# Softcap attention and a two-layer network on one core: P kept in f32 for two more pairs, exponentials turned unscaled, split scores on row halves, the cap in registers

## The chip, the cores and the metric

One Trainium2 chip, one of its cores. The time is the device time of one execution in microseconds (us). The kernel before takes 695.26 us (median of 3 runs, 694.31 to 695.97). Engines in the text: PE is TensorE, DVE VectorE, ACT ScalarE, POOL GpSimd, SP the engine that issues the DMAs.

## The reference, cut to what matters

```
q, k, v: (4, 12, 448, 64) f32            # batch, heads, tokens, head width
s = q @ k.T / 8;  s = cap * tanh(s / cap)
p = exp(s - max(s));  p = p / (sum(p) + 1e-9)
x = p @ v, heads side by side            # (4*448, 768)
h = x @ w_in                             # 768 -> 2048
g = where(h > 0, h, alpha * h)           # alpha per column of h
out = g @ w_out                          # 2048 -> 768
```

## The kernel before, in words

Every product has to come out with the accuracy of f32. The kernel has two ways to get it. Either the operands stay f32 and PE takes several passes over each product (a product is then two matmul records in the trace), or each operand is split into an f16 high part and an f16 low part (`hi`, `lo`) and PE forms three f16 products (high by high, high by low, low by high).

The work is 12 units in batch 0 (6 pairs of heads by two parts of the tokens, 384 and 64 of them: `PART`) and 18 units in batches 1 to 3 (one pair of heads with all 448 tokens each). `steps` (L532) goes through a unit in steps of two blocks of 128 rows of scores (one head each); the last step of a 448-token unit has one block that holds 64 rows of each head. A step is: scores on PE, tanh on ACT (L553), row maxima on DVE (L558), the bias of the exponential (L560), exponential with its row sums on ACT (L565), then 1/sum on POOL and DVE (L570, L573), and then P is turned, since P @ V needs P with the keys on the partitions.

- Scores of batches 0 and 1 are f32 (`scores_32`, L520): a head's 64 columns of q and k stand on one half of PE's rows, and the two heads' products are meant to run side by side. In batches 2 and 3 q and k are split, and `nat` holds (q high, q low), (k high, k high), (k low, k low); one DMA transpose makes `qkTs` of it, and `split_scores` (L780) makes two matmuls of all 128 rows per block (L785).
- P of batch 0 is turned on PE by `turn_32` (L602): four f32 matmuls of P by a diagonal matrix of 1/sum, `diags` (made at L607), so that the turn also divides. The turned P is copied from PSUM (L621), and `PV_32` (L657) multiplies it by V in f32.
- P of batches 1 to 3 is scaled, split into f16 high and low (`turn_split`, L582) and turned by DMA (L598); V is split (`split_v`), and `PV_split` (L642) makes 24 f16 matmuls per unit.

Each unit's output is scaled and split by `xout` into `xring`, and the network goes on from there: `mm1` (L806) is x @ w_in, `mm2` (L847) is g @ w_out, both in three f16 products. The weights are loaded, put together as f32 (L902 to L912), bounded by their column norms (`norms`, L919: products on PE, L926, and a maximum on DVE, L931), scaled and split.

The order on each engine is written out ahead of time: every operation is recorded with a priority, a dependency list and an assumed duration, and `Plan.order` (L133) runs through them and gives each free engine the ready operation of lowest priority. The constants at the top of the file (`PEN`, `B0_P`, ...) and the table `OFF` shift the priorities. Where the plan sees PE without work ahead of `FILL_END`, it puts in a filler, a matmul of the identity by itself (`fill`, L1063) that nobody reads.

Of the kernel before, what the change touches and what calls it, by code (L numbers as in the profile page):

```python
# [24 lines left out]
GUARD = 1e-9 * math.exp(EXP_BIAS)  # L25
PD_A = 6
PD_B = 6
MQ = 3
AQ = 3
PEN = 4509.92  # L30
PEN2 = -1345.18
PENP = 6482.25
B0_P = -50.35
LD_P = -35.85
LO_P = 301.38
MM_P = 3324.02
X_P = 53.71
ST_P = 19.81
ST1_P = 13.45
PV_P = 374.14  # L40
QK_P = -32.7
V_P = -1.09
WI_P = 40.03
WI_S = -0.97
A_S = 13.05
MM1_P = 198.89
WO_P = 329.05
WO_S = -16.5
WT_P = -1461.61
WT_S = -141.91  # L50
B1_P = 277.05
B_S = 241.79
EVAC_P = -145.66
# [14 lines left out]
QA = 0.5  # L68
VA = 1.0
FS = [0, 6]  # L70
TURN = 95.0
TURN_P = 905.0
SCORE = 1040.0
# [5 lines left out]
OFF = [34.6, 0.4, 29.9, -6.1, 0.0, 1.5, -90.6, 40.5, 0.0, 0.0, -257.7, 0.0, 2.6, -1.0, 26.8, -8.5, -42.6, 107.4, 10.3, 125.2, 8.6, -267.5, -58.1, 2.0, -9.3, 235.7, 4.8, -32.5, 207.0, 194.2, 463.8, 229.6, 0.0, -31.2, -255.6, -6.9, -24.3, 57.8, -178.1, 70.7, 0.0, 225.2, -115.2, -52.7, 0.0, -130.7, 63.2, 240.7, 63.4, -111.4, 0.0, 0.0, 9.4, 97.8, -60.1, -181.2, -100.1, -35.7, 137.8, 0.0, -6.1, -78.0, -257.2, 31.2, -2.2, -147.9, 21.3, -0.4, 0.0, 21.9, 119.4, -148.7, 89.0, -63.5, 14.5, 76.1, -40.7, -49.1, 31.5, -2.8, 125.9, -8.9, 99.3, -23.6, -83.9, 175.4, 11.7, 163.5, -170.9, 0.0, 13.5, 0.2, -5.3, 0.2, -132.0, -577.9, -1.6, 9.7, -185.1, -10.0, 15.0, -245.3, 0.0, -22.7, 32.7, 149.3, -1091.5, -40.3, 0.0, -672.3, 15.6, -127.9, -897.3, 55.4, -59.5, 0.0, 167.9, 2.2, 12.5, -39.1, 123.8, -60.7, -437.0, -54.8, -543.8, -541.5, 4.4, 0.0, -1.4, -92.4, -0.7, -60.4, 150.0, 75.5, -504.3, 26.7, 69.5, 182.6, -11.4, -57.0, 55.8, 95.6, -4.2, 2.6, 230.8, 0.0, -572.4, 62.6, 1.6, -54.4, 0.0, -3.0, 20.2, 99.9, 396.1, 2.6]  # L79
# [9 lines left out]
class Plan:  # L89
# [43 lines left out]
    def order(self):  # L133
# [8 lines left out]
        port = {"dve": 0.0, "pool": 0.0}  # L142
# [46 lines left out]
        while todo:  # L189
# [10 lines left out]
            for e in free:  # L200
# [3 lines left out]
                while ready[e]:  # L204
# [20 lines left out]
                    elif e == "pe":  # L225
                        free[e] = run_pe(t, o.rows)
# [36 lines left out]
def kernel(  # L263
# [72 lines left out]
    nat = ct([P, 6 * NCH, P], F16, "nat")  # L336
    qkTs = ct([P, 2, 6 * NCH, CP], F16, "qkTs")
    aux = qkTs[:, 1].rearrange("p g t -> p (g t)").bitcast(F32)
    qzs = [aux[:, :512], aux[:, 512:1024]]
    qzr = [(("qkT", 1), 0, 512), (("qkT", 1), 512, 1024)]  # L340
# [3 lines left out]
    diags = ct([P, 4, P], F32, "diags")  # L344
# [4 lines left out]
    ams = ct([P, 3, 8], F32, "ams")  # L349
    vam = ct([P, 2, 2 * NPAIR], F32, "vam")  # L350
# [111 lines left out]
    def vbatch(b):  # L462
# [18 lines left out]
        first, *rest = pow2(u.inv, u.s, None)  # L481
        allmax(prio, u.vmx, P, [(u.tok, 6, 7)], first, [(u.tok, 7, 9)])
# [49 lines left out]
    def steps(u, prio, n, S_, s_ns, sr_, scale, dma):  # L532
# [4 lines left out]
        for i0 in range(0, nb, 2):  # L537
# [15 lines left out]
            op(pr, {"act": 245 + 377 * m}, lambda e, s=s, t=t, m=m: nc.scalar.activation(  # L553
                out=t, in_=s[:, :m, :S].rearrange("p c (j k) -> p c j k", j=NCH), func=AF.Tanh, scale=scale[0]),
# [47 lines left out]
    def turn_32(u, pr, n, c, t, tr, f, fr):  # L602

        i = dg_no[0] % 4
        dg_no[0] += 1
        d, dr = diags[:, i], ("dg", i, i + 1)
        op(pr, either(P, f=True, pool=True), lambda e: scaled(e, d, ident, f), r=[identr, fr], w=[dr])  # L607
        h = plan.handle("a")

        def turn_P(e):  # L610
# [24 lines left out]
    def split_v(u, prio, rv, rvt):  # L635
        vs = vs16[:CP, u.idx % 2]
        vt = [(("vs", u.idx % 2), z, z + 1) for z in range(2)]
# [4 lines left out]
    def PV_split(u, prio, n, vs, vt):  # L642
# [11 lines left out]
        op(prio, {"pe": TURN + 12 * (n / 2.4 + 12)}, PV, r=vt + [("pt", u.po[x], u.po[x] + 4 * n) for x in range(2)], w=[h])  # L654
        return h

    def PV_32(u, prio, n, vt, vr):  # L657
        h = plan.handle("a")

        def PV(e):  # L660
            pv = ps_p[h.slot]
# [6 lines left out]
        op(prio, {"pe": 4 * (n / 0.6 + 30) + 50}, PV, r=[("pt", u.po[0], u.po[0] + 8 * n), vr, (vb[u.b].tok, 7, 9)], w=[h], rows=0.875)  # L668
        return h
# [15 lines left out]
    def attention32(part, pair):  # L685
# [18 lines left out]
        op(prio, {"pe": TURN + 205 * nch}, lambda e, h=h: turn(h, rq, c0, nch), r=[rqr, identr], w=[h, qr], rows=0.7)  # L704
        op(prio, either(n, True), lambda e, h=h: copy(e, qz, ps_p[h.slot][:, o - c0 * CP:o - c0 * CP + n]), r=[h], w=[qr], port=False)
        dma = pair >= (PD_A, PD_B)[part]
# [4 lines left out]
        else:  # L711
            u.po = [po, po + n]
            u.pt = pt32[:CP, po:po + 8 * n].rearrange("p (j t) -> p j t", j=NCH)
            u.pv = [u.pt[:, :, y * n:(y + 1) * n] for y in range(2)]
        steps(u, prio, n, scores_32(qz, kt[:, pair], n), lambda blocks: SCORE, [qr, ktr], [icap], dma)
# [8 lines left out]
        else:  # L724
            xout(u, prio + X_P, h, n, o, vb[0].s, [(vb[0].tok, 7, 9)])


    def attention(b, pair):
# [11 lines left out]
        qkT = qkTs[:, u.idx % 2]  # L740
        qt = (("qkT", u.idx % 2), 0, 1344)
        if scores32:
            both = qkT.rearrange("p g t -> p (g t)").bitcast(F32)
            qz, kz = both[:, :S], both[:, S:2 * S]
            for i, raw, rr_, dst in ((14, rk, rkr, kz), (13, rq, rqr, qz)):
                h = plan.handle("a")
                w = (qt[0], (i - 13) * S, (i - 12) * S)
                op(prio - i, {"pe": TURN + 205 * NCH}, lambda e, h=h, raw=raw: turn(h, raw, 0, NCH), r=[rr_, identr], w=[h, w], rows=0.7)
                op(prio - i, either(S, True), lambda e, h=h, dst=dst: copy(e, dst, ps_p[h.slot][:, :S]), r=[h], w=[w], port=False)
        else:  # L750
# [10 lines left out]
            nq, nk, nl = (nat[:CP, 2 * NCH * i:2 * NCH * (i + 1)] for i in range(3))  # L761
            q4, k4 = (t.rearrange("p (c d) -> p c d", d=D) for t in (rq, rk))
            nt = [("nat", i * 512, i * 512 + 512) for i in range(3)]
            pr = prio - 13
            split(pr, q4, rqr, s[:CP, 0:1], amt, nq[:, :, 0:D], nt[0], nq[:, :, D:], nt[0], share(2 * u.idx, QA))
# [342 lines left out]
```

## Time and profile before

| | |
|---|---|
| median of 3 runs | 695.26 us |
| the profiled execution | 696.31 us, of which the span from first to last instruction 694.5 us |
| PE busy | 680.4 us, 98% of the span |
| DVE, ACT, POOL busy | 486.9, 420.7, 265.0 us |
| granted TensorE clock | 0.999 of full speed |

A share of busy time counts an engine that has at least one instruction under way, so a pipelined PE is busy from the start of one matmul to the end of the next. What one matmul costs in a row of them is read from the starts in the timeline.

### The profile page before, as it was taken

How to read it: one execution, taken by the hardware profiler on the slowest of the kernel's cores; microseconds unless marked ns; L12 is line 12 of the kernel's file. 1: busy time of each engine (PE TensorE's matmuls, PEld its weight loads, DVE VectorE, ACT ScalarE, POOL GpSimd, SP SyncE). 2: the span in 40 equal slices, each digit the busy share in tenths (PEclk: the TensorE clock that was granted, in tenths of full speed). 3: DMA queues.
4: the chain of work that ended last, by engine and by line, in shares of the span. 5: the costliest groups of instructions: out<-in, count | busy, mean ns of one | idle time of the engine just before them, and what ended most of it. 6: DMA issues, size and time to landing. Idle time of an engine off the chain costs nothing.

```text
span 694.5 us, 13601 instructions
## 1 busy us (share of the span) xinstructions
PE 680.4 (98%) x5122; PEld 433.6 (62%) x5122; DVE 486.9 (70%) x953; ACT 420.7 (61%) x828; POOL 265.0 (38%) x405
## 2 busy tenths in 40 slices
PE   8999999999999998999999999999999999999997
PEld 6888887898786555544555555545455555555664
DVE  4899999999989987786886858588688503441000
ACT  5789889777777765773785656477668602331100
POOL 1343366565476662373663524256245200000000
PEclk9999999999999999999999999999999999999999
DMA  9996652975973599867669998596487710000011
GB/s 222 251 324 185 178 196 87 241 151 162 187 158 73 108 195 201 181 112 119 114 119 189 206 181 177 116 159 119 83 159 134 146 33 24 0 1 1 24 40 29
DMA packets 207393, 93.50 MB, mean 135 GB/s; under 512 B 170912, under 2 KB 203616, under 8 KB 207328
## 3 DMA queue, kind: packets, MB, share of 16 engines
q1 hardware_dynamic: 207328, 92.64, 61.9%
q8 instruction: 40, 0.66, 0.4%
q14 instruction: 25, 0.20, 0.1%
HBM read 45.82 MB, written 5.51 MB: 74 GB/s over the span
## 4 chain that ended last, share of the span: by engine, by line
PE 80%; DMA 9%; DVE 5%; ACT 3%; issue 2%; POOL 1%; SPq 1%; ACTq 0%; DVEq 0%; POOLq 0%
PE p L847 29%; PE p L806 24%; PE p L612 6%; DMA ptall<-pw 5%; PE s L785 5%; PE p L651 5%; PE s L528 4%; PE p L665 3%; PE p L490 2%; DMA wp<-in_moe_w_out_dram 2%; PE p L926 1%; DMA qkTs<-nat 1%; DMA nat<-in_v_dram 1%; DVE mxs L558 1%; PE p L390 1%
## 5 line engine op out<-in xcount | busy, mean ns | idle before, releaser
L847 PE MATMUL p<-wp,gall 128*128 128x384 f16 x1344 | 225.7, 326 | 0.0
L806 PE MATMUL p<-xring,wi 128*128 128x448 f16 (+2 forms) x1440 | 225.2, 315 | 0.0
L806 PEld LDWEIGHTS <-wi 128*128 128x128 f16 x1440 | 134.5, 98 | 84.5 <-issue 4.6
L847 PEld LDWEIGHTS <-gall 128*128 128x128 f16 x1344 | 129.7, 98 | 88.5 <-issue 4.1
L565 ACT ACTIVATE tall<-tall,mxs,small 128x448 f32<-128x448 f32 x126 | 94.5, 751 | 23.7 <-POOL mxs L560 14.9
L816 DVE SCALAR_TENSOR_TENSOR gr<-p,ca_g,gr 128x448 f32<-128x448 f32 (+2 forms) x80 | 46.6, 585 | 52.1 <-ACT gr L406 51.9
L558 DVE TENSOR_REDUCE mxs<-tall 128x2 f32<-128x896 f32 x72 | 68.4, 960 | 11.5 <-ACT tall L553 11.2
L406 ACT ACTIVATE gr<-p,cs_g 128x448 f32<-128x448 f32 (+2 forms) x67 | 36.7, 548 | 58.6 <-PE p L806 55.9
L560 POOL TENSOR_SCALAR mxs<-mxs,small 128x2 f32<-128x2 f32 (+1 forms) x68 | 30.4, 448 | 86.9 <-DVE mxs L558 81.3
L570 POOL TENSOR_SCALAR rr<-sums 128x2 f32<-128x2 f32 x96 | 35.2, 367 | 51.8 <-ACT tall L565 35.0
L416 DVE SCALAR_TENSOR_TENSOR pw<-tall,rr,pw 128x448 f16<-128x448 f32 x63 | 46.1, 732 | 6.8 <-ACT pw L406 4.8
L406 ACT ACTIVATE wp<-p,small 128x384 f32<-128x384 f32 x20 | 11.5, 577 | 64.4 <-PE p L847 64.4
L651 PE MATMUL p<-ptall,vs 112*64 112x448 f16 x432 | 45.5, 354 | 1.7 <-DMA ptall<-pw 1.2
L553 ACT ACTIVATE tall<-s,ams 128x896 f32<-128x896 f32 (+1 forms) x48 | 42.3, 901 | 6.1 <-PE s L785 3.5
L413 POOL TENSOR_TENSOR pw<-tall,pw 128x448 f16<-128x448 f32 x35 | 39.8, 1137 | 13.3 <-ACT pw L400 11.0
L400 ACT ACTIVATE gall<-gr 128x384 f16<-128x384 f32 (+4 forms) x55 | 25.4, 467 | 28.2 <-DVE gr L816 27.8
L785 PE MATMUL s<-qkTs 128*128 128x448 f16 (+1 forms) x192 | 38.1, 355 | 2.7 <-ACT tall L553 2.2
L413 POOL TENSOR_TENSOR gall<-gr,gall 128x256 f16<-128x256 f32 (+4 forms) x42 | 33.2, 794 | 13.7 <-ACT gall L400 10.3
L406 ACT ACTIVATE pw<-tall,rr 128x448 f16<-128x448 f32 x43 | 28.5, 663 | 15.6 <-DMA ptall<-pw 11.9
L651 PEld LDWEIGHTS <-vs 112*64 112x64 f16 x432 | 24.3, 110 | 20.7 <-issue 6.0
L612 PE MATMUL p<-diags,gall 128*112 128x128 f32 x280 | 36.0, 278 | 0.5 <-POOL diags L408 0.5
L402 POOL CAST gall<-gr 128x192 f16<-128x192 f32 (+4 forms) x32 | 22.7, 711 | 34.6 <-DVE gr L816 33.9
(155 smaller groups left out, 1000.6 us busy)
## 6 DMA issues: line engine op xcount, KB each, us to landing
wp<-in_moe_w_in_dram SPq DMA_DIRECT2D x16, 768.0 KB, 8.0
wp<-in_moe_w_out_dram SPq DMA_DIRECT2D x16, 768.0 KB, 5.1
rvs<-in_v_dram SPq DMA_DIRECT2D x38, 224.0 KB, 3.5
rqk<-in_q_dram SPq DMA_DIRECT2D x18, 224.0 KB, 3.4
rqk<-in_k_dram SPq DMA_DIRECT2D x18, 224.0 KB, 3.3
ptall<-pw SPq DMA_TRANSPOSE x144, 3.3
wp<-in_k_dram SPq DMA_DIRECT2D x6, 224.0 KB, 9.0
wp<-in_q_dram SPq DMA_DIRECT2D x6, 224.0 KB, 8.0
```

The costliest lines, as they stand in the source:

```text
L406: nc.scalar.activation(out=o, in_=i, func=AF.Copy, scale=s)
L413: (nc.gpsimd if e == "pool" else nc.vector).tensor_tensor(out=o, in0=a, in1=b, op=ALU.subtract)
L416: nc.vector.scalar_tensor_tensor(out=o, in0=i, scalar=s, in1=hi, op0=ALU.mult, op1=ALU.subtract)
L553: op(pr, {"act": 245 + 377 * m}, lambda e, s=s, t=t, m=m: nc.scalar.activation(out=t, in_=s[:, :m, :S].rearrange("p c (j k) -> p c j k", j ...
L558: op(pr, {"dve": 136 + 469 * m}, lambda e, mt=mt, t=t: nc.vector.tensor_reduce(out=mt, in_=t, axis=AX.XY, op=ALU.max), r=tr, w=[mr], port= ...
L565: nc.scalar.activation(out=t[:, x], in_=t[:, x], func=AF.Exp, scale=capt, bias=mt[:, x:x + 1], accum_out=u.sums[:, c:c + 1])
L612: nc.tensor.matmul(ps_p[h.slot][:CP, j * P:(j + 1) * P], t[:, j], d, start=True, stop=True)
L651: nc.tensor.matmul(pv[x * D:(x + 1) * D, :n], vs[:, z, c:c + D], u.pt[x][:CP, y * NCH + kc], start=(i == 0), stop=(i == len(prods) - 1))
L785: nc.tensor.matmul(s[rows, i, :S], qT[:, x * S + cols.start:x * S + cols.stop], qkT[:, r0:r0 + NCH, :], start=(z == 0), stop=(z == 1))
L806: nc.tensor.matmul(ps_p[h.slot][:, :n], w[:, z, kk, :], x[:, d, o:o + n], start=(kk == 0 and z == d), stop=(kk == NPAIR - 1 and z == 1))
L816: op(pr, {"dve": 198 + 1.07 * n}, lambda e: nc.vector.scalar_tensor_tensor(out=t, in0=ps_p[h.slot][:, :n], scalar=ca_g[:, j:j + 1], in1=t, ...
L847: nc.tensor.matmul(ps_p[h.slot][:, :NH], g[j][:, d, t * P:(t + 1) * P], w[:, z, hf * NH:(hf + 1) * NH], start=(j == 0 and z == d), stop=(j ...
```

## The change

Five edits, and a new set of constants.

1. P of all batch 0 units, and of the first two pairs of batch 1 (`FP = [0, 2]`), goes through `turn_32` without scaling: the four matmuls by `diags` become four `nc.tensor.transpose` of the exponentials, as they are (`TU_A`, `TU_B` = 6 leave no unit scaled). 1/sum is taken once for all blocks of a unit. In `PV_32` the factors 1/sum are spread over the 64 columns of a head by f32 matmuls with the identity, multiplied by V's scale on the way out of PSUM (`R` in the new tile `xs`), and the product P @ V is multiplied by R in a new `xout_32`.
2. The two pairs of batch 1 no longer split P and V, and don't turn P by DMA.
3. `split_scores` makes three products of 64 rows (q high by k high, q low by k high, q high by k low), the two heads on the two halves of PE's rows; `nat` and the DMA transpose shrink from 24 to 16 groups, the copy of k's halves (L768) goes, and q and k are all split the direct way, the low part head by head (`QA = 1.0`, `heads`).
4. The scale of tanh (batches 0 and 1) and of every exponential is read from an ACT register (`capr`, `icapr`) in place of a column of SBUF.
5. The maximum over the weights' norm products is taken by ACT, one per chunk of 128 columns, into `junk` (`NM = 1.0`).

`qkTs` has three buffers, V of batch 0 lies in other places before use, and the constants and `OFF` have new values, so the whole order is drawn anew.

```diff
-QA = 0.5
+QA = 1.0
 FS = [0, 6]
+FP = [0, 2]
...
     def turn_32(u, pr, n, c, t, tr, f, fr):
-        i = dg_no[0] % 4
-        d, dr = diags[:, i], ("dg", i, i + 1)
-        op(pr, either(P, f=True, pool=True), lambda e: scaled(e, d, ident, f), r=[identr, fr], w=[dr])
+        d, dr = ident, identr
+        if u.scaled:
...
         def turn_P(e):
             for j in range(NCH):
-                nc.tensor.matmul(ps_p[h.slot][:CP, j * P:(j + 1) * P], t[:, j], d, start=True, stop=True)
+                o = ps_p[h.slot][:CP, j * P:(j + 1) * P]
+                if u.scaled:
+                    nc.tensor.matmul(o, t[:, j], d, start=True, stop=True)
+                else:
+                    nc.tensor.transpose(o, t[:, j], ident)
...
     def PV_32(u, prio, n, vt, vr):
+        f, (R, rt), _ = rr[:, u.idx % 3], *xs_parts(u, n)
+            def factors(e):
+                for c in range(2 * n // P):
+                    for y, rows, cols in spans(n, c):
+                        nc.tensor.matmul(ps_p[h.slot][y * D:(y + 1) * D, cols], f[:, c:c + 1].to_broadcast([P, D]), ident[:, rows], start=True, stop=True)
+            op(prio, either(n, True, f=True), lambda e: scaled(e, R, ps_p[h.slot][:, :n], vb[u.b].s), ...)
...
+    def xout_32(u, prio, h, n, o):
+        op(prio, {"dve": 160 + 1.04 * n}, lambda e: nc.vector.tensor_tensor(out=t, in0=ps_p[h.slot][:, :n], in1=R, op=ALU.mult), ...)
+        op(prio, either(n, pool=True), lambda e: copy(e, hi, t), ...)
+        op(prio, diff(n, False), lambda e: minus(e, lo, t, hi), ...)
...
         def split_scores(s, blocks):
-            for i, c in enumerate(blocks):
-                for z in range(2):
+            for z, y in ((0, 2), (1, 2), (0, 3)):
+                for i, c in enumerate(blocks):
                     for x, rows, cols in spans(S, c):
-                        r0 = 2 * NCH * (1 + z) + x * NCH
-                        nc.tensor.matmul(s[rows, i, :S], qT[:, x * S + cols.start:x * S + cols.stop], qkT[:, r0:r0 + NCH, :],
-                                         start=(z == 0), stop=(z == 1))
+                        a = slice(x * D, (x + 1) * D)
+                        nc.tensor.matmul(s[rows, i, :S], qT[a, z * S + cols.start:z * S + cols.stop], qT[a, y * S:(y + 1) * S],
+                                         start=(z == 0 and y == 2), stop=(y == 3))
...
+    capr, icapr = (nc.scalar.alloc_register(x) for x in ("capr", "icapr"))
+    nc.scalar.load(capr, capt[:1].bitcast(I32))
+    nc.scalar.load(icapr, icap[:1].bitcast(I32))
```

In all, PE's program goes from 136 fillers to 39, from 168 products by `diags` to 224 transposes, from 432 to 384 matmuls of `PV_split`, from 192 to 288 of `split_scores`, and has 64 products of factors and 16 more f32 products of P @ V.

PE's order in batch 0, a few steps after its start (L612 turns P, L528 are scores, `gall` is where the exponentials of batch 0 lie, `s` and `p` are PSUM tiles), before:

```order
L612 MATMUL p_65<-diags,gall 112x128 x4
L612 MATMUL p_66<-diags,gall 112x128 x4
L528 MATMUL s_61<-tall,qkTs 128x224 x4
L1063 LDWEIGHTS ident
L1063 MATMUL p_65<-ident 128x128
L612 MATMUL p_63<-diags,gall 112x128 x4
L387 MATMUL p_64<-ident,vam 1x128
L528 MATMUL s_62<-tall,qkTs 64x224 x4
L390 MATMUL p_64<-mxt,ones 128x1
```

and now (L654 turns P, L557 are scores, L519 turns q and k, L711 spreads the factors):

```order
L654 MATMUL p_65<-ident,gall 112x128 x4
L654 MATMUL p_63<-ident,gall 112x128 x4
L654 MATMUL p_66<-ident,gall 112x128 x4
L557 MATMUL s_61<-tall,qkTs 128x224 x4
L557 MATMUL s_62<-tall,qkTs 64x224 x4
L711 MATMUL p_64<-ident,rr 64x128 x2
L711 MATMUL p_64<-ident,rr 64x64 x2
L519 MATMUL p_65<-ident,wp_100 64x112 x4
```

The four products by `diags` of a block are four transposes by the identity, and the product of factors stands ahead of each unit's P @ V.

PE's order at the first P @ V of batch 1 (L651 is `PV_split`, `vs` the split V), before:

```order
L926 MATMUL p_64<-wp_94 128x128
L926 LDWEIGHTS wp_94
L926 MATMUL p_64<-wp_94 128x128
L651 LDWEIGHTS vs_118
L651 MATMUL p_65<-ptall,vs_118 64x448
```

and now (L722 is `PV_32`, `rvs` V as it was loaded, `tall` where the exponentials of batch 1 lie):

```order
L885 MATMUL p_64<-xring,wi_86 128x192
L711 MATMUL p_66<-ident,rr 64x128 x6
L711 MATMUL p_66<-ident,rr 64x64 x2
L412 MATMUL p_65<-ident,vam 1x128
L654 MATMUL p_63<-ident,tall 112x128 x4
L557 MATMUL s_61<-qkTs 128x224 x4
L722 MATMUL p_64<-ptall,rvs 64x448 x8
L415 MATMUL p_65<-mxt,ones 128x1
L654 MATMUL p_63<-ident,tall 112x128 x4
```

The 24 f16 matmuls of the unit are 8 f32 products, its factors come ahead of them, and the turns of the next unit stand around them.

PE's order at the first matmul of `mm2` (its row has `gall` and a weight tile `wp`), before and, below, now:

```order
L1063 LDWEIGHTS ident
L1063 MATMUL p_63<-ident 128x128
L847 LDWEIGHTS gall
L847 MATMUL p_65<-wp_101,gall 128x384
L847 LDWEIGHTS gall
```

```order
L693 LDWEIGHTS vs_118
L693 MATMUL p_66<-ptall,vs_118 64x448
L926 LDWEIGHTS gall
L926 MATMUL p_65<-wp_101,gall 128x384
L926 LDWEIGHTS gall
```

The 67 fillers that stood ahead of `mm2` are gone; a `PV_split` is followed by `mm2` at once.

## Rows read from the trace of the kernel before

**Rows 1.** The page, busy time of each engine, PE's line.

```profile
PE 680.4 (98%) x5122; PEld 433.6 (62%) x5122; DVE 486.9 (70%) x953; ACT 420.7 (61%) x828; POOL 265.0 (38%) x405
```

**Rows 2.** Windows of the span: length, then busy time of PE, PEld, DVE, ACT, POOL, clock, DMA.

```profile
17.50:130.00 112.50, 112.14 (x1168) 92.05 (x1169) 108.03 (x203) 96.12 (x204) 54.91 (x85) 1.00 0.71 206
130.00:200.00 70.00, 69.43 (x755) 59.65 (x754) 65.14 (x122) 50.28 (x107) 39.19 (x55) 1.00 0.83 183
200.00:217.00 17.00, 15.37 (x193) 12.31 (x190) 16.29 (x38) 14.50 (x28) 13.37 (x18) 1.00 0.48 91
217.00:360.00 143.00, 139.50 (x860) 75.76 (x859) 116.51 (x226) 97.87 (x187) 75.64 (x111) 1.00 0.74 139
```

**Rows 3.** Timeline of PE at `mm2`'s start: start us, length us, line, operation.

```profile
211.58 3.02 PE L1063 MATMUL p<-ident 128*128 128x128 f16 x51
216.05 1.05 PE L1063 MATMUL p<-ident 128*128 128x128 f16 x16 [1.46 <-DVE xring L416]
216.94 2.11 PE L847 MATMUL p<-wp,gall 128*128 128x384 f16 x12
```

**Rows 4.** Groups of PE's matmuls by form: count, busy us, mean ns.

```profile
L612 PE MATMUL p<-diags,gall 128*112 128x128 f32 x280 | 36.0, 278 | 0.5 <-POOL diags L408 0.5
L387 PE MATMUL p<-ident,n_wi 128*4 128x128 f32 x4 | 1.1, 272 | 0.0
```

**Rows 5.** Timeline of PE, a stretch of turned P in batch 0.

```profile
69.86 1.13 PE L612 MATMUL p<-diags,ptall 128*112 128x128 f32 x8
70.82 1.91 PE L612 MATMUL p<-diags,gall 128*112 128x128 f32 x16
...
75.28 1.03 PE L528 MATMUL s<-tall,qkTs 64*128 64x224 f32 x8
...
77.95 1.95 PE L665 MATMUL p<-ptall,nat 112*64 112x256 f32 x16
```

**Rows 6.** Timeline of PE, first products of batch 0, and a row of fillers.

```profile
5.38 2.80 PE L490 MATMUL p<-ident,wp 112*64 112x112 f32 x40 [0.34 <-DMA wp<-in_k_dram]
8.12 1.03 PE L528 MATMUL s<-tall,qkTs 64*128 64x224 f32 x8
9.07 0.60 PE L490 MATMUL p<-ident,wp 112*64 112x112 f32 x8
9.61 2.83 PE L528 MATMUL s<-tall,qkTs 64*64 64x224 f32 x24
...
22.66 1.11 PE L1063 MATMUL p<-ident 128*128 128x128 f16 x17
23.71 1.52 PE L665 MATMUL p<-ptall,nat 112*64 112x192 f32 x16
```

**Rows 7.** Timeline of PE, split scores and P @ V of batches 2 and 3.

```profile
298.68 0.57 PE L785 MATMUL s<-qkTs 128*64 128x448 f16 x4
299.18 3.58 PE L806 MATMUL p<-xring,wi 128*128 128x448 f16 x18
...
302.69 2.46 PE L651 MATMUL p<-ptall,vs 112*64 112x448 f16 x24
305.09 13.79 PE L806 MATMUL p<-xring,wi 128*128 128x448 f16 x72
...
326.34 1.68 PE L785 MATMUL s<-qkTs 128*128 128x448 f16 x8
327.95 0.38 PE L390 MATMUL p<-mxt,ones 2*128 2x2 f32 x2
```

**Rows 8.** Groups by form on DVE and ACT: busy us, mean ns.

```profile
L370 DVE TENSOR_REDUCE n_wi<-p 128x4 f32<-128x512 f32 x8 | 5.4, 680 | 0.1
L768 DVE COPY nat<-nat 112x1024 f16<-112x1024 f16 x12 | 9.1, 760 | 0.1
L406 ACT ACTIVATE gr<-p,cs_g 128x448 f32<-128x448 f32 x37 | 23.4, 633 | 47.3 <-PE p L806 46.4 <-PE p L387 0.8
L400 ACT ACTIVATE tall<-p 128x448 f32<-128x448 f32 x4 | 2.2, 543 | 6.1 <-PE p L490 6.1
```

More of the change, by code (lines that the diff above doesn't have):

```diff
@@ L25 @@
 GUARD = 1e-9 * math.exp(EXP_BIAS)
+VM = 0
+NM = 1.0
+TU_A = 6
+TU_B = 6
 PD_A = 6
@@ L29 @@
 AQ = 3
[L30 to L53, printed above, removed]
+PEN = 12239.75
+PEN2 = -1123.94
+PENP = 4140.94
+B0_P = 55.77
+LD_P = -94.66
+LO_P = 968.21
+MM_P = 7639.04
+X_P = 235.33
+ST_P = 9.35
+ST1_P = -53.75
+PV_P = 594.03
+QK_P = -169.88
+V_P = 110.22
+WI_P = 94.37
+WI_S = -30.28
+A_S = 5.6
+MM1_P = 304.75
+WO_P = -57.62
+WO_S = 104.91
+WT_P = -403.33
+WT_S = 169.86
+B1_P = 691.46
+B_S = 235.54
+EVAC_P = -1182.76
 LAT = 35.0
@@ L225, in order @@
                     elif e == "pe":
-                        free[e] = run_pe(t, o.rows)
+                        free[e] = run_pe(t + (SWITCH if o.mode and o.mode != mode else 0.0), o.rows)
+                        mode = o.mode
                         end = free[e] + DRAIN
@@ L335 @@
     rvs = ct([P, 2, 2 * NCH * D], F32, "rvs")
[L336 to L340, printed above, removed]
+    NQK = 4 * NCH
+    nat = ct([P, NATS * NQK, P], F16, "nat")
+    qkTs = ct([P, 3, NQK, CP], F16, "qkTs")
+    aux = qkTs[:, 2].rearrange("p g t -> p (g t)").bitcast(F32)
+    qzs = [aux[:, i * 256:(i + 1) * 256] for i in range(2)]
+    qzr = [(("qkT", 2), i * 256, (i + 1) * 256) for i in range(2)]
     ident, identr = ct([P, P], F32, "ident"), ("ident", 0, 1)
@@ L481, in vbatch @@
         first, *rest = pow2(u.inv, u.s, None)
+        if b < VM:
+            first, *rest = root(u.inv, lambda: nc.vector.reciprocal(out=u.s, in_=u.inv))
         allmax(prio, u.vmx, P, [(u.tok, 6, 7)], first, [(u.tok, 7, 9)])
@@ L636, in split_v @@
         vs = vs16[:CP, u.idx % 2]
-        vt = [(("vs", u.idx % 2), z, z + 1) for z in range(2)]
+        vt = [("vs", u.idx % 2 * 2 + z, u.idx % 2 * 2 + z + 1) for z in range(2)]
         sv, st = vb[u.b].s[:CP], (vb[u.b].tok, 7, 9)
@@ L666, in PV @@
                                      start=(kc == 0), stop=(kc == NCH - 1))
-        op(prio, {"pe": 4 * (n / 0.6 + 30) + 50}, PV, r=[("pt", u.po[0], u.po[0] + 8 * n), vr, (vb[u.b].tok, 7, 9)], w=[h], rows=0.875)
-        return h
+        op(prio, {"pe": 4 * (n / 0.6 + 20)}, PV, r=[("pt", z, z + 3 * u.js + n) for z in u.po] + [vr], w=[g_], rows=0.875, mode=1)
+        return g_
+    def xout_32(u, prio, h, n, o):
+        x, ((R, rt), (t, tt)) = xring[:, xslot(u.b, u.pair)], xs_parts(u, n)
+        hi, lo = x[:, 0, o:o + n], x[:, 1, o:o + n]
+        op(prio, {"dve": 160 + 1.04 * n}, lambda e: nc.vector.tensor_tensor(out=t, in0=ps_p[h.slot][:, :n], in1=R, op=ALU.mult),
+           r=[h, rt], w=[tt], port=False)
+        op(prio, either(n, pool=True), lambda e: copy(e, hi, t), r=[tt], w=[xr(u.b, u.pair, 0, o, n)])
+        op(prio, diff(n, False), lambda e: minus(e, lo, t, hi), r=[tt, xr(u.b, u.pair, 0, o, n)], w=[xr(u.b, u.pair, 1, o, n)])
     def xout(u, prio, h, w, o, sc, sr=()):
@@ L712, in attention32 @@
             u.po = [po, po + n]
-            u.pt = pt32[:CP, po:po + 8 * n].rearrange("p (j t) -> p j t", j=NCH)
-            u.pv = [u.pt[:, :, y * n:(y + 1) * n] for y in range(2)]
-        steps(u, prio, n, scores_32(qz, kt[:, pair], n), lambda blocks: SCORE, [qr, ktr], [icap], dma)
+            u.js = 2 * n
+            u.ph = pt32[:CP, po:po + 8 * n].rearrange("p (j h t) -> p j h t", j=NCH, h=2)
+            u.pv = [u.ph[:, :, y] for y in range(2)]
+        steps(u, prio, n, scores_32(qz, kt[:, pair], n), SCORE, [qr, ktr], [icap], dma)
         vt, vr = v0[0, pair]
@@ L764, in attention @@
+            nt = [("nat", n0 * P // 2 + i * 256, n0 * P // 2 + i * 256 + 256) for i in range(4)]
+            q4, k4 = (t.rearrange("p (h c d) -> p h c d", h=2, d=D) for t in (rq, rk))
             pr = prio - 13
-            split(pr, q4, rqr, s[:CP, 0:1], amt, nq[:, :, 0:D], nt[0], nq[:, :, D:], nt[0], share(2 * u.idx, QA))
-            split(pr, k4, rkr, s[:CP, 1:2], amt, nk[:, :, 0:D], nt[1], nl[:, :, 0:D], nt[2], share(2 * u.idx + 1, QA))
-            both = nat[:CP, 2 * NCH:]
-            op(pr, {"dve": 420}, lambda e: nc.vector.tensor_copy(both[:, :, D:], both[:, :, 0:D]), w=[nt[1], nt[2]])
@@ L769, in attention @@
-            op(pr, {"sp": (3920, 2100, 2350)}, lambda e: nc.sync.dma_start_transpose(out=qkT, in_=nat[:CP].rearrange("p g d -> p (g d)")),
-               r=nt, w=[qt])
+            split(pr, q4, rqr, s[:CP, 0:1], amt, parts[0], nt[0], parts[1], nt[1], share(2 * u.idx, QA), range(2))
+            split(pr, k4, rkr, s[:CP, 1:2], amt, parts[2], nt[2], parts[3], nt[3], share(2 * u.idx + 1, QA), range(2))
+            op(pr, {"sp": (2630, 2100, 1570)}, lambda e: nc.sync.dma_start_transpose(
+                out=qkT, in_=nat[:CP, n0:n0 + NQK].rearrange("p g d -> p (g d)")), r=nt, w=[qt])
```

161 lines of the change are left out of this document (106 added, 55 removed).

## The prediction

> **What bounds the kernel now.** The page comes first: PE is busy for 680.4 us of a span of 694.5 us, DVE for 487 [rows 1]. A busy PE need not be useful, so the windows come next [rows 2]. From 17.5 to 217 us PE idles for only 2.6 us (0.36, 0.57 and 1.63), but DVE idles for only 10 us there (189.5 busy of 199.5): two engines are full at once. From 217 to 360 us PE idles for 3.5 us and DVE has room. The timeline then shows what the busy share hides: ahead of `mm2`, from 211.58 to 216.94 us, PE runs 67 fillers and waits 1.46 us more, so 5.4 us in which nothing of use is done [rows 3]. Outside of such places PE's own work sets the end. I therefore price the change by what PE's program gains and loses, then ask whether DVE lets PE go at that pace. The rows sum to the profiled execution, 696.31 us, which is 1.05 us above the median of the runs.
>
> **Turning P in batch 0.** From 69.86 to 75.28 us stand 48 records of L612 (two of the rows between are left out), that is 24 products or six turns: 0.113 us a record, 0.226 a product, 0.904 a turn [rows 5]. The 42 turns cost 38.0 us. A transpose of f32 data is in the trace too: L387 transposes 128x128 f32 in one record, 272 ns against 278 for one record of L612 [rows 4]. So I price a transpose as one of the two records, 0.113 us. 168 of them cost 19.0 us: 19.0 saved. The bounds: a transpose that streams as fast as a filler of the same 128 columns (17 from 22.66 to 23.71, 0.062 each [rows 6]) saves 27.6; one that costs as much as the product saves nothing.
>
> **Spreading the factors.** New are 48 products of 64x128 and 16 of 64x64, f32 onto half of PE's columns. The nearest row is L490, f32 onto half the columns, 112 wide: 20 products (40 records) from 5.38 to 8.12 us, 0.137 each, which makes 0.157 for 128 and 0.078 for 64 [rows 6]. Together 8.8 us added. Bounds: one record of L612 per 128 columns gives 6.3, two give 12.7.
>
> **Two pairs of batch 1.** 14 turns of four transposes add 6.3 us (bounds 3.5 and 12.7, as above). Their P @ V in f32: 8 products of 256 columns take 1.95 us at most [rows 5], so 448 columns take 3.4; `PV_split` takes 2.40 (302.69 to 305.09) [rows 7]. That adds 2.0 for the two. Their DMA transposes and splits go; they stood beside other work and I count nothing for them on PE's path. If that cover were gone, it would show as a gain only.
>
> **Split scores.** Before, a two-block step is 0.805 us (326.34 to 327.95 for two), a single-block step 0.50 (298.68 to 299.18) [rows 7]. After, six matmuls in three pairs. That two row halves run together shows in batch 0: four f32 products, eight records of 224 columns, take 0.95 us (8.12 to 9.07) [rows 6]; one after another, at L612's 0.113 us for 128 columns, they would take 8 x 0.198 = 1.58. Three f16 pairs stream 3 x 448 columns where those stream 4 x 448, which makes 0.71; at `PV_split`'s pace of 0.10 a matmul [rows 7] it is 0.60. I take 0.70, from the row with the same tiling. 36 steps save 3.8 us and 12 single steps lose 2.4: net 1.4 saved. Bounds: 0.60 saves 6.2; halves that don't overlap (six at 0.20) cost 23.1.
> The Trainium skill (TensorEngine Tiling (Array Packing), Restrictions and Gotchas) says that different row tiles cannot use the same PSUM bank at the same time. In the single-block step both halves write one bank. By the rule those 12 steps would go one after another, 1.21 us each, and the sum would be 6.1 us higher. The row disagrees: the 64-row steps of batch 0 write both halves to one bank too, and three of them take 2.83 us, 0.94 each [rows 6], no more than the two-bank ones.
>
> **Fillers.** 97 go, at 0.062 us [rows 6]: 6.0 us, of which 67 are the ones ahead of `mm2`. This is a gain only if PE has work in their place, and not a wait.
>
> **Other engines.** DVE loses the norm maxima (8 at 680 ns, 5.4 us) and the copy of k (12 at 760 ns, 9.1 us) [rows 8], half of the P splits of two pairs and some reciprocals; it gains the low parts of q and k in two pieces and all of them, some 14 us, after 217 us where it has room. ACT gets 32 maxima in exchange, and saves on 168 exponentials and 48 tanh what a scale from SBUF costs, 90 ns by a pair of like rows (633 against 543) [rows 8]: 19 us. ACT is 61% busy and its queue ends no wait of length on PE, so I count zero, between 0 and 2 us gained.
>
> **The sum.** -19.0 + 8.8 + 6.3 + 2.0 - 1.4 - 6.0 = -9.3 us. 696.31 - 9.3 - 1.05 = 686.0 us. What is late next is the chain through DVE into `mm2` and into the first units of batch 1.
>
> **Rivals.**
> 1. DVE sets the pace to 217 us, and PE waits where the fillers stood. For it: DVE is 95% busy there, and the first units of batch 1 are drawn earlier. Against: DVE drops the 5.4 us of norms and more in just that stretch. The fillers' 6.0 us come back as idle: 692.0 us.
> 2. The new order also clears what PE idles between 200 and 360 us (5.1 us [rows 2]), and the split scores reach 0.60 (4.8 more): 676 us. For it: P of the f32 units needs no DMA and no reciprocal before its turn. Against: idle of that kind falls where a plan with assumed durations misses, and a new plan misses elsewhere.
> 3. Slower: the f16 row halves do not run side by side. Place: the 48 steps of `split_scores`. Price: 23.1 lost in place of 1.4 gained, 710.5 us. It decides from the point where a step takes 0.70 + 9.3/48 = 0.89 us. Against it stands the f32 pair above; for it, that no f16 pair on row halves is in this trace. A transpose at the full price of a product would end in the same region (19.0 + 6.3 lost, 711), and one record in L387 speaks against it.
> 4. The clock. Granted clock is 1.00 in every window to 360 us [rows 2], with L612 at work in batch 0; this trace has no stretch at 1.2 GHz to price a fall with. A fall over the 224 transposes alone would double their 25.3 us, 711 us. Runs of transposes are short (three in a row in the order shown) and f32 scores stand between them.
> The Trainium skill (TensorE: Matmul & The Clock Gate, Part 4) says that transposes do not count as busy for the clock; only if that starves the clock does rival 4 come true, and no run here shows it either way yet.
>
> **Chances.** Forecast (681 to 689) 0.50; rival 1 (689 to 694) 0.24; rival 2 (below 681) 0.13; rivals 3 and 4 with a full-price transpose 0.09; no change to speak of 0.04. A measurement of this kernel tells about 0.2% from no change, 1.4 us. A little of rival 1 lies within that, so: faster 0.85, same 0.06, slower 0.09. The range takes in rivals 1 and most of 2, 677 to 695.
>
> **What would show it.** In the profile after: L654 at about 0.45 us a turn; L711 at 0.16 a product; a two-block step of L860 near 0.70 and a single one like it; no or few fillers after 17 us and `mm2` starting near 210 us with PE busy before it. Rival 1 shows as PE idle released by DVE or POOL between 100 and 260 us, rival 3 as L860 steps over 0.89, rival 4 as a clock under 0.95 in a window of batch 0. The prediction is wrong if PE's idle after 17 us grows by more than 6 us, or if a transpose takes two records.

## The result and the profile after

The changed kernel takes 688.47 us (median of 4 runs, 688.11 to 690.01) against 695.62 us of the kernel before (694.31 to 696.48, 4 runs): ratio 0.9903, 95% interval 0.9881 to 0.9926. The forecast was 686.0 us, faster; the range of 677 to 695 holds it. That is 1.0% less, and the interval leaves out 1. The profiled execution is the one of 688.11 us, span 686.3 us: 8.2 us less than the profiled one before.

The page's line of busy times, which answers to [rows 1]:

```profile
PE 670.5 (98%) x5121; PEld 413.8 (60%) x5121; DVE 477.9 (70%) x945; ACT 400.6 (58%) x867; POOL 227.0 (33%) x355
```

PE is busy for 9.9 us less and idle for 1.7 us more (686.3 - 670.5 = 15.8, before 694.5 - 680.4 = 14.1). That is the whole 8.2 us. The windows, columns as in [rows 2], show where the idle went:

```profile
17.50:130.00 112.50, 109.51 (x1202) 86.70 (x1204) 108.03 (x196) 93.43 (x233) 50.88 (x70) 1.00 0.74 223
130.00:200.00 70.00, 67.66 (x686) 53.03 (x683) 63.91 (x111) 51.08 (x135) 38.39 (x50) 1.00 0.59 142
200.00:217.00 17.00, 16.64 (x147) 12.77 (x146) 16.17 (x40) 13.20 (x29) 9.86 (x16) 1.00 0.55 87
217.00:360.00 143.00, 141.14 (x901) 74.93 (x896) 121.06 (x243) 92.63 (x182) 58.58 (x98) 1.00 0.73 135
```

From 17.5 to 217 us PE idles for 5.7 us in place of 2.6; from 217 to 360 us for 1.9 in place of 3.5. The clock is 1.00 in all four. Of PE's groups by form (count, busy us, mean ns), those that answer to the terms of the sum:

```profile
L654 PE MATMUL p<-ident,gall 128*112 128x128 f32 x140 | 20.2, 280 | 0.0
L654 PE MATMUL p<-ident,tall 128*112 128x128 f32 x56 | 8.7, 278 | 1.1 <-ACT tall L594 0.9
L711 PE MATMUL p<-ident,rr 128*64 128x128 f32 x96 | 8.1, 285 | 0.0
L722 PE MATMUL p<-ptall,rvs 112*64 112x448 f32 x32 | 6.4, 542 | 0.0
L860 PE MATMUL s<-qkTs 64*128 64x448 f16 x216 | 24.8, 351 | 1.5 <-ACT tall L582 0.8 <-DMA qkTs<-nat 0.7
```

L654 has 140 + 56 records here (and 28 more for `ptall`), one for each of 224 transposes: a transpose is one record, as L387's row let expect [rows 4]. The timeline of PE (start us, length us) shows what a turn, the factors and a step of split scores cost from one start to the next:

```profile
15.49 0.65 PE L654 MATMUL p<-ident,gall 128*112 128x128 f32 x4
16.07 0.60 PE L519 MATMUL p<-ident,wp 112*64 112x112 f32 x8
...
20.17 1.52 PE L654 MATMUL p<-ident,gall 128*112 128x128 f32 x12
21.62 1.93 PE L557 MATMUL s<-tall,qkTs 64*128 64x224 f32 x16
23.49 0.55 PE L711 MATMUL p<-ident,rr 128*64 128x128 f32 x8
23.87 0.56 PE L519 MATMUL p<-ident,wp 112*64 112x112 f32 x8
...
260.62 0.74 PE L860 MATMUL s<-qkTs 64*128 64x448 f16 x6
261.30 0.38 PE L415 MATMUL p<-mxt,ones 2*128 2x2 f32 x2
...
265.61 0.76 PE L860 MATMUL s<-qkTs 64*64 64x448 f16 x6
266.30 2.12 PE L926 MATMUL p<-wp,gall 128*128 128x384 f16 x12
```

A turn by itself takes 0.58 us and three together 1.45, that is 0.48 each; four products of factors take 0.38, 0.095 each; a two-block step of split scores takes 0.68 and a single-block step 0.69. `mm2` starts no earlier:

```profile
215.72 2.46 PE L693 MATMUL p<-ptall,vs 112*64 112x448 f16 x24
218.11 2.12 PE L926 MATMUL p<-wp,gall 128*128 128x384 f16 x12
```

It starts at 218.11 us, before at 216.94 [rows 3]. The fillers ahead of it are gone, and other work stands there: from 17.5 to 217 us PE is busy for 193.8 us with 5 fillers (0.3 us) where it was busy for 196.9 with 100 (6.2 us, at 0.062), so 2.8 us more of other work in the same stretch. What ended PE's waits in that stretch, by the profile's view of waits (line, releaser, us in total, times, longest):

```profile
PE p L693 <- DMA ptall<-pw: 1.2, 1, 1.2
PE s L557 <- ACT gall L582: 1.1, 1, 1.1
PE p L654 <- ACT tall L594: 0.9, 1, 0.9
PE p L412 <- DVE vam L506: 0.8, 1, 0.8
PE p L415 <- DVE mxt L410: 0.7, 2, 0.4
PE p L885 <- DVE gr L895: 0.5, 1, 0.5
PE s L557 <- ACT tall L582: 0.2, 1, 0.2
```

ACT ends 2.2 us of them, DVE 2.0 and a DMA 1.2: no single engine holds PE up.

### The profile page after: what moved, and what is told of

Its sections match the earlier page's. It is cut to its first block, busy times and chain, and to the rows that moved or that the text cites. A ratio compares the mean times of both kernels' runs of the same rounds, so it can differ in the third digit from the quotient of the medians.

```text
span 686.3 us, 13473 instructions
## 1 busy us (share of the span) xinstructions
PE 670.5 (98%) x5121; PEld 413.8 (60%) x5121; DVE 477.9 (70%) x945; ACT 400.6 (58%) x867; POOL 227.0 (33%) x355
## 5 line engine op out<-in xcount | busy, mean ns | idle before, releaser
L594 ACT ACTIVATE tall<-tall,mxs 128x448 f32<-128x448 f32 x126 | 82.9, 660 | 22.5 <-POOL mxs L589 18.0
L587 DVE TENSOR_REDUCE mxs<-tall 128x2 f32<-128x896 f32 (+1 forms) x72 | 68.2, 960 | 14.5 <-ACT tall L582 14.2
L589 POOL TENSOR_SCALAR mxs<-mxs,small 128x2 f32<-128x2 f32 (+1 forms) x77 | 38.5, 500 | 105.1 <-DVE mxs L587 94.0
L438 POOL TENSOR_TENSOR gall<-gr,gall 128x192 f16<-128x192 f32 (+4 forms) x47 | 37.3, 795 | 29.0 <-ACT gall L425 26.3
L606 POOL TENSOR_SCALAR rr<-sums 128x2 f32<-128x2 f32 (+3 forms) x78 | 31.2, 400 | 44.0 <-ACT tall L594 28.2
L441 DVE SCALAR_TENSOR_TENSOR pw<-tall,rr,pw 128x448 f16<-128x448 f32 x56 | 39.0, 698 | 5.0 <-ACT pw L431 2.7
L860 PE MATMUL s<-qkTs 64*128 64x448 f16 (+1 forms) x288 | 33.3, 353 | 1.5 <-ACT tall L582 0.8
L438 DVE TENSOR_TENSOR gall<-gr,gall 128x384 f16<-128x384 f32 (+4 forms) x65 | 28.7, 444 | 4.5 <-ACT gall L425 1.7
L438 DVE TENSOR_TENSOR pw<-tall,pw 128x448 f16<-128x448 f32 x34 | 21.7, 644 | 13.7 <-ACT pw L425 10.7
L438 POOL TENSOR_TENSOR pw<-tall,pw 128x448 f16<-128x448 f32 x22 | 24.6, 1120 | 17.5 <-ACT pw L425 16.6
```

The lines of the kernel that those rows point to most:

```text
L438: (nc.gpsimd if e == "pool" else nc.vector).tensor_tensor(out=o, in0=a, in1=b, op=ALU.subtract)
L441: nc.vector.scalar_tensor_tensor(out=o, in0=i, scalar=s, in1=hi, op0=ALU.mult, op1=ALU.subtract)
L587: op(pr, {"dve": 136 + 469 * m}, lambda e, mt=mt, t=t: nc.vector.tensor_reduce(out=mt, in_=t, axis=AX.XY, op=ALU.max), r=tr, w=[mr], port= ...
L589: op(pr, {"dve": 200, "pool": 265}, lambda e, mt=mt: (nc.gpsimd if e == "pool" else nc.vector).tensor_scalar(out=mt, in0=mt, scalar1=ncap, ...
L860: nc.tensor.matmul(s[rows, i, :S], qT[a, z * S + cols.start:z * S + cols.stop], qT[a, y * S:(y + 1) * S], start=(z == 0 and y == 2), stop= ...
```

## The experiments

Each is an edit of the changed kernel; medians stand beside its 688.47 us. A ratio is to the kernel before, run beside that edit; where a difference is small, the ratio is to be held against the changed kernel's 0.9903 (0.9881 to 0.9926). The theories: A, TensorE's own work sets the end; B, up to 217 us VectorE sets the pace (B' in its later form: both are full); C, ScalarE's latency counts; D, what idle is left lies in the drawn order.

**The turn as a product.**

```diff
-                    nc.tensor.transpose(o, t[:, j], ident)
+                    nc.tensor.matmul(o, t[:, j], ident, start=True, stop=True)
```

> The changed kernel with one word undone: the 224 turns are again f32 matmuls by the identity, still unscaled, in the same order on every engine. Theory A, TensorE's own work sets the end: a turn takes 0.90 us as in the kernel before, where the changed kernel shows 0.48 (three in a row) to 0.58 (one alone), so 56 x 0.32 to 0.42 = 18 to 24 us more, 706 to 712 us. Theory B, TensorE waits for VectorE up to 217 us whatever it does there: the longer turns fill waits, under 8 us more, below 697 us.

Measured: 707.09 us (706.07 to 709.45), 18.6 more; ratio to before 1.0164 (1.0140 to 1.0188). PE's busy time is 697.0 us, 26.5 more. Its window over the crowded stretch:

```profile
17.50:217.00 199.50, 198.92 (x2086) 164.02 (x2086) 172.49 (x302) 145.29 (x358) 87.08 (x119) 1.00 0.58 172
```

PE is idle for 0.6 us there, in place of 5.7: the longer turns first fill the waits, then push the end. Theory A holds. The transposes alone are worth more than the whole change gives; without them the kernel is slower than the one before.

**No f32 pairs in batch 1.**

```diff
-FP = [0, 2]
+FP = [0, 0]
-FILL_END = 365429.37
+FILL_END = 20000.0
```

> The changed kernel with batch 1's two pairs back on split P and DMA turns, and no fillers after 20 us. TensorE loses 14 turns (7 us), two sets of factors (1.5) and 1.6 of P @ V: 10 us of work. Theory A, only TensorE's own work counts: 688 - 10 = 678 us. Theory B, the two f32 pairs are paid for because VectorE and the DMAs set the pace of the first units of batch 1: TensorE idles 20 us or more between 150 and 260 us and the time is above the kernel before, 697 to 715 us.

Measured: 708.15 us (707.75 to 710.45), ratio 1.0193 (1.0168 to 1.0219). The windows where it is lost:

```profile
180.00:190.00 10.00, 6.10 (x72) 4.48 (x69) 9.88 (x16) 7.96 (x17) 8.29 (x11) 1.00 1.01 236
190.00:200.00 10.00, 5.07 (x31) 2.84 (x33) 9.67 (x16) 5.68 (x17) 4.16 (x5) 0.64 0.87 212
210.00:220.00 10.00, 7.24 (x37) 4.00 (x39) 9.58 (x18) 8.23 (x26) 6.45 (x9) 0.50 0.68 133
230.00:240.00 10.00, 6.50 (x23) 2.59 (x22) 9.96 (x13) 6.78 (x10) 4.54 (x4) 0.50 0.29 54
```

PE (first number) is busy for half to three quarters of each window shown, DVE (third) for 96% and more, and the granted clock falls from 1.00 to 0.50, its lower level of 1.2 GHz. Theory A alone fails: the time is 30 us above its 678. PE idles for 23.8 us between 150 and 260 us, as theory B asked. But the cause is not VectorE alone by this run. From 175 to 245 us VectorE ends 12.9 us of PE's waits, ScalarE 7.0 and GpSimd 3.8; VectorE is busy for 56.9 us of the 60 from 180 to 240, hardly more than the 56.1 of the changed kernel. Two more things differ besides the pairs: the order is drawn anew, and the clock. PE is busy for 672.6 us, 2.1 more than in the changed kernel, with about 10 us less work as the expectation prices it, so some 12 of the 20 us may be the clock's (an estimate). That the two pairs buy off VectorE is likely, not shown.

**The halves one after the other, and both heads on one half.** The first edit orders a step's matmuls as three for one half, then three for the other; the second leaves the order and puts all on rows 0 to 63, so that both heads get head 0's scores.

```diff
# halves in turn
-            for z, y in ((0, 2), (1, 2), (0, 3)):
-                for i, c in enumerate(blocks):
-                    for x, rows, cols in spans(S, c):
+            for i, c in enumerate(blocks):
+                for x, rows, cols in spans(S, c):
+                    for z, y in ((0, 2), (1, 2), (0, 3)):
# one half
-                        a = slice(x * D, (x + 1) * D)
+                        a = slice(0, D)
```

> The changed kernel with the split scores' six matmuls of a step in another order: three for one row half, then three for the other, so that neighbours use the same half. If side by side means pairs of neighbours on different halves (the forecast's reading), the pairs go one after another: a step takes 6 x 0.19 = 1.1 to 1.2 us in place of 0.68, 48 steps, 20 to 25 us more, 708 to 713 us. If TensorE looks further ahead than the neighbour, or if the halves never ran together, no change: 688 us.

Measured: 689.29 us (688.51 to 689.92), ratio 0.9909 (0.9887 to 0.9932): no change that the intervals show. A step, from its timeline:

```profile
261.63 0.75 PE L860 MATMUL s<-qkTs 64*128 64x448 f16 x6
262.31 0.38 PE L415 MATMUL p<-mxt,ones 2*128 2x2 f32 x2
```

0.68 us, as before. That left two readings, which the next run told apart.

> The changed kernel with all six matmuls of a split-score step on rows 0 to 63 (both heads then get head 0's scores). If the two halves run side by side, whatever the order within a step (what the run with the halves in turn leaves possible), a two-block step takes 6 x 0.19 = 1.1 to 1.2 us in place of 0.68 and 36 steps cost 16 to 19 us, 704 to 707 us (the single steps still have two column halves). If a matmul of 64 rows takes half the time by itself, nothing changes: 688 us.

Measured: 707.06 us (706.71 to 708.26), ratio 1.0159 (1.0107 to 1.0210). A two-block step and a single-block step:

```profile
262.84 1.31 PE L860 MATMUL s<-qkTs 64*128 64x448 f16 x6
264.08 0.38 PE L415 MATMUL p<-mxt,ones 2*128 2x2 f32 x2
...
268.39 0.76 PE L860 MATMUL s<-qkTs 64*64 64x448 f16 x6
269.08 2.12 PE L926 MATMUL p<-wp,gall 128*128 128x384 f16 x12
```

The two-block step takes 1.24 us: six matmuls on one half go one after another. So the halves do run side by side in the changed kernel, and they do so even with three matmuls of one half ahead of the other's first. The single-block step stays at 0.69: there the two heads also stand on different column halves, and that alone is enough. PE's busy time rises by 20.0 us (690.5) and the time by 18.6: theory A once more.

**The cap from a column.**

```diff
-                ..., func=AF.Tanh, scale=icapr if scale[0] is icap else scale[0]),
+                ..., func=AF.Tanh, scale=scale[0]),
-                    nc.scalar.activation(..., func=AF.Exp, scale=capr,
+                    nc.scalar.activation(..., func=AF.Exp, scale=capt,
```

> The changed kernel with the scale of tanh and of the exponentials read from an SBUF column again, same order on every engine. ScalarE's busy time rises by about 216 x 0.09 = 19 us in all. Theory A: ScalarE is off the path, 0 to 1.5 us more, 688 to 690 us. Theory C, the latency of a step counts because units are drawn early: TensorE waits for exponentials and tanh, 3 to 8 us more, 691 to 696 us.

Measured: 691.70 us (690.91 to 693.37), 3.2 more; ratio 0.9949 (0.9930 to 0.9967). An exponential by group, in this run and in the changed kernel:

```profile
L594 ACT ACTIVATE tall<-tall,mxs,small 128x448 f32<-128x448 f32 x126 | 94.4, 752 | 23.2 <-POOL mxs L589 18.6 <-DVE mxs L589 4.5
```

```profile
L594 ACT ACTIVATE tall<-tall,mxs 128x448 f32<-128x448 f32 x126 | 82.9, 660 | 22.5 <-POOL mxs L589 18.0 <-DVE mxs L589 4.2
```

92 ns each, as priced by the pair of like rows, and 16.0 us of ScalarE in all (416.6 against 400.6; the forecast had 19). But it is not free: 3.2 us of it reach the end, though ScalarE is at 58%, and the ratio's interval lies above the changed kernel's. PE's waits that ACT ends grow from 3.7 to 6.1 us over the whole run, its idle from 15.8 to 18.0. My zero for this edit (0 to 2) was too low; theory C holds at its lower end.

**The norms' maxima on VectorE.**

```diff
-NM = 1.0
+NM = 0.0
```

> The changed kernel with the maxima of the weights' norms back on VectorE: 8 x 0.68 = 5.4 us more there, 32 x 0.46 = 15 us less on ScalarE; the order is drawn anew from the same constants, with 97 fillers in place of 39. Theory B' (after the first runs: up to 217 us TensorE and VectorE are both full, and what VectorE gets there TensorE waits for): 3 to 6 us more, 691 to 695 us. Theory A, only TensorE's work counts: 58 fillers that stand in waits, 688 to 690 us.

Measured: 695.92 us (693.12 to 697.85, 12 runs), ratio 0.9999 (0.9975 to 1.0023), 7.4 more, above both theories. The order is drawn anew, and the profiled run (693.20 us) has 3.9 us more of PE busy, about what 58 fillers come to (3.6 at 0.062), and 1.2 us more of idle. It doesn't tell VectorE's work from the order's, so what the fifth edit gives by itself stays open.

**VectorE's load, with and without a new order.** Left out whole (order drawn anew), cut to 2 columns, and done twice (both in the same order):

```diff
# left out
-            op(prio, {"dve": 945}, lambda e: nc.vector.scalar_tensor_tensor(
-                out=f, in0=lo, scalar=29, in1=f, op0=ALU.logical_shift_right, op1=ALU.bitwise_or), r=[sr], w=[fr])
# 2 columns
+                out=f[:, :2], in0=lo[:, :2], scalar=29, in1=f[:, :2], op0=ALU.logical_shift_right, op1=ALU.bitwise_or), r=[sr], w=[fr])
# twice
+            op(prio, {"dve": 945}, lambda e: [nc.vector.scalar_tensor_tensor(
+                out=f, in0=lo, scalar=29, in1=f, op0=ALU.logical_shift_right, op1=ALU.bitwise_or) for _ in range(2)], r=[sr], w=[fr])
```

> The changed kernel without the instruction that puts the low word of the weights in place (L991, 32 x 0.95 = 30 us of VectorE, most of it before 200 us; the weights then lack their low bits). TensorE's work is the same. Theory B': TensorE's 5.7 us of idle from 17.5 to 217 us shrink, 683 to 686 us, and no more than that since TensorE's own work then sets the pace alone. Theory A in its strict form: 688 us. If VectorE alone set the pace up to 217 us: 675 us or less.

Measured: 695.94 us (692.85 to 697.86, 12 runs), ratio 0.9990 (0.9962 to 1.0018): slower by 7.5 us (6.1 by the ratios) with less to do. All theories missed it. PE idles for 21.3 us (span 695.4, busy 674.1), spread over eleven kinds of waits of 0.6 to 2.2 us each and some shorter ones. Hence the next two, which keep the order.

> The changed kernel with the low word of the weights put in place on 2 of 768 columns only (L991, 32 instructions; the weights lack their low bits elsewhere): some 28 us less on VectorE, nearly all before 210 us, and, other than the run without the instruction, the same order on every engine. Theory B', VectorE's pace is what TensorE waits for up to 217 us: the 5.7 us of idle there go, 682 to 685 us. Theory D, the idle comes from places where the drawn order misses, not from how much VectorE has to do: 687 to 690 us.

> The changed kernel with that instruction done twice (the second time changes nothing): 30 us more on VectorE, nearly all before 210 us, same order otherwise. VectorE has 10 to 11 us of idle from 17.5 to 217 us. Theory B', both engines are full: 15 to 30 us more, 703 to 718 us. Theory A, only TensorE's work counts: under 5 us more.

Measured: 2 columns 686.94 us (686.46 to 687.33), ratio 0.9892 (0.9878 to 0.9906); twice 714.85 us (714.10 to 716.46), ratio 1.0297 (1.0279 to 1.0314). The stretch from 17.5 to 217 us, first with 2 columns, then twice, and a window of the latter:

```profile
17.50:217.00 199.50, 194.81 (x2044) 153.34 (x2044) 167.68 (x347) 159.76 (x399) 85.27 (x137) 1.00 0.66 183
```

```profile
17.50:217.00 199.50, 174.59 (x1803) 135.53 (x1800) 193.61 (x320) 135.81 (x341) 85.58 (x111) 0.97 0.59 169
120.00:130.00 10.00, 7.09 (x63) 5.32 (x64) 9.97 (x15) 4.32 (x7) 2.51 (x2) 0.69 0.48 145
```

With 20 us less on VectorE there (167.7 against 188.1) PE still idles for 4.7 us in place of 5.7, and the time falls by 1.5 by the medians, 0.8 by the ratios, whose intervals overlap: a gain is not shown. 686.94 lies a hair below theory D's 687 to 690 and above B''s 682 to 685, and the idle that stays speaks for D. With 31 us more in the whole run (508.7 against 477.9) the time rises by 26.4. A reserve of 4 to 5 us on VectorE, with the rest paid in full, would give that; one load doesn't show where the payment starts. A part of the 26.4 may be the clock's: it falls to 0.69 in the window shown, where PE waits 2.9 us for VectorE, and PE's busy time grows by 6.3 us (676.8) with the same program. Most of PE's waits in the stretch are ended by VectorE here, the longest kinds (5.5 and 5.2 us) by the doubled instruction itself. So TensorE leads in the changed kernel, and VectorE is right behind it.

**The old priorities, and the same without fillers.** All priority constants and `OFF` of the kernel before; then that order with the fillers after 8 us not issued.

```diff
-PEN = 12239.75
+PEN = 4509.92
...
-OFF = [135.9, 60.2, ...
+OFF = [34.6, 0.4, ...
# and, without fillers
-                    started.append((now, lambda _, slot=banks[-1]: self.fill(slot), e))
+                    started.append((now, (lambda _, slot=banks[-1]: self.fill(slot)) if now < 8000.0 else (lambda _: None), e))
```

> The changed kernel with the priority constants and the OFF table of the kernel before: the same work on TensorE but for 119 fillers in place of 39 (5 us). If the gain is the work that TensorE lost (theory A), it stays within 5 us of the changed kernel, 688 to 694 us. If the new priorities carry the gain, it is lost: 697 us or more.

> The run with the old priorities, same order, without the 87 fillers after 8 us (5.4 us of TensorE). If they stand where TensorE would wait anyway: 686 to 688 us, the idle takes their place. If the real engines are ahead of the plan there: 681 to 684 us, below both kernels. If the clock falls for want of them: 690 us or more, and a window below 0.95.

Measured: old priorities 686.93 us (686.67 to 689.03), ratio 0.9863 (0.9813 to 0.9913); without fillers 687.66 us (686.32 to 689.92), ratio 0.9911 (0.9893 to 0.9929). The gain does not come from the new priorities. Without fillers PE is busy for 5.9 us less (669.6 against 675.6), and in the profiled runs, of which the first is its kernel's slowest, it idles for 3.8 us more (15.5 against 11.6). By the medians nothing is gained, so the fillers stood in waits for the most part. Neither run is told apart from the changed kernel by its interval.

**A third f32 pair.**

```diff
-FP = [0, 2]
+FP = [0, 3]
```

> The changed kernel with a third pair of batch 1 in f32 (FP = [0, 3], order drawn anew, still 39 fillers). TensorE gets 7 turns (3.5 us), factors (0.8) and 0.8 of P @ V: 5 us more; VectorE, GpSimd and the DMAs lose the pair's splits and turns. Theory A, only TensorE's work counts once the two pairs are in: 692 to 695 us. Theory B', VectorE is still what TensorE waits for: 688 us or less.

Measured: 690.60 us (690.19 to 690.93), ratio 0.9919 (0.9896 to 0.9942), 2.1 more by the medians, 1.1 by the ratios: between the theories. PE is busy for 4.4 us more (674.9) and idles for 1.9 us less. Its interval overlaps the changed kernel's, so that a third pair costs anything is not shown.

## Why the prediction was right, point by point

- **The bound.** TensorE's own work: shown, with VectorE close behind it. Where PE's program grew in the same order (turns as products, one half), the time rose by 18.6 us for 26.5 and 20.0 us of busy time. Where VectorE's work fell by 20 us in the crowded stretch, the time fell by 0.8 to 1.5, which the intervals don't tell from none; where it grew by 31, the time rose by 26.4.
- **The terms.** By PE's busy groups before and after, and from start to start. A group's busy time counts the tails of its runs, which the next matmul covers; the last column leaves them out: for each line it adds up the times from one matmul's start to the next one's, waits left out.

| term | forecast us | busy groups us | start to start us |
|---|---|---|---|
| turns, batch 0 and two pairs | -19.0 + 6.3 = -12.7 | 43.4 to 32.7: -10.7 | 40.2 to 28.6: -11.6 |
| factors | +8.8 | +10.4 | +7.6 |
| P @ V | +2.0 | 66.0 to 66.9: +0.9 | 63.7 to 64.5: +0.8 |
| split scores | -1.4 | 38.5 to 33.9: -4.6 | 34.5 to 31.5: -3.0 |
| fillers | -6.0 | 10.7 to 4.3: -6.4 | 10.1 to 4.1: -6.0 |
| sum | -9.3 | -10.4 | -12.2 |

  The turn came out at 0.48 to 0.58 us and not at the 0.45 of the records alone. A product of factors took 0.095 in a row of four, less than the 0.157 taken from L490. The split scores gained more than forecast, though the step by itself was forecast well (0.68 and 0.69 for 0.70): two two-block steps in a row take 1.24 us. P @ V in f32 cost less than forecast. So the priced terms gave 2.9 us more than the sum, and lines that the sum doesn't name took 2.4 us more than before (the f32 scores and x @ w_in 0.7 each). That the two nearly cancel is luck.
- **The fillers' term** was half a gain. Of the 6.0 us, 3.1 came back as idle from 17.5 to 217 us; the rest is the 2.8 us of other work done there. The profiled execution missed the sum by 1.1 us (8.2 for 9.3): PE idles for 1.7 us more in all and is busy for 0.6 less than the sum has it. The median missed it by 2.5, and the runs spread over 1.9; the other 1.4 us are that the profiled execution lies 1.05 above the median before and 0.36 below it after. The forecast of `mm2` at 210 us was wrong: the order had other work ahead of it.
- **Rival 1** came half true in its cost and not in its cause. Its sign was idle ended by DVE or POOL between 100 and 260 us; DVE ends 0.4 us there and POOL none, ACT and the DMAs 3.7. That VectorE would set the pace but for the two f32 pairs is likely by the run without them, but that run has another order and a lower clock. Less work on VectorE did not take the waits away; what is left are single waits on several engines, which the drawn order misses.
- **Rival 2** came true only between 217 and 360 us (1.6 us of idle less). **Rival 3** did not: 0.68 us a step. In the single-block step both halves write one bank, and it takes 0.69. The rule of the Trainium skill (TensorEngine Tiling (Array Packing), Restrictions and Gotchas) does not show here, with tiles that differ in their column halves too. **Rival 4** did not: clock 1.00 in each window with transposes. What the Trainium skill (TensorE: Matmul & The Clock Gate, Part 4) says of transposes and the clock decides nothing here, among the other matmuls of this order.
- **ScalarE at zero** was the step that failed. The forecast read that its queue ends no wait of length on PE. The trace before has 2.2 us of them, on the tanh of a step:

```profile
PE s L785 <- ACT tall L553: 2.2, 2, 1.8
```

  The 16 us are worth 3.2 us on the path when they are put back. If they gave as much when they were taken away, the sum should have been 3.2 us lower; that the 3.1 us of idle in the fillers' place made up for it is luck.

## What to carry to other kernels

When two engines are full in one stretch, price a change on both: 10 us of extra TensorE work for the f32 pairs was probably the cheaper side, since the run without them was 20 us slower, though with another order and a lower clock. Here 31 us of added load cost 26, and 20 us taken away from the same stretch gave 1.5 by the medians, which is within the noise, so a reserve is bounded by adding, not by taking away. And compare single edits in the same order: a redrawn one moved this kernel by 6 to 7 us the wrong way with less work in it.

## What was not expected of the hardware

Matmuls on the two row halves of TensorE run side by side even when three of one half stand ahead of the first of the other: 0.68 us a step in either order, 1.24 when all use one half. Where the two also stand on different column halves, one row half does as well: 0.69 with both row halves and with one.
